# The end of a fused attention and Fourier kernel: when the last output products are made, and on which engine the last sums are

## The chip, the cores and the metric

The kernel runs on one core of one Trainium2 chip. The metric is the device time of one execution in microseconds (us). The kernel before takes 426.28 us (median of 3 runs, 426.26 to 426.36). The page of the profile and all answers of the trace come from one more execution of the same program, taken by the hardware profiler.

## The reference, cut to what matters

One input x of 2048 tokens and 448 features goes through two branches, and a gate mixes them.

```python
# x: (1, 2048, 448), 16 heads of 28 features
g = sigmoid((x * gate_w).sum(-1, keepdims=True))
qkv = (x @ wqkv).reshape(B, S, 3, 16, 28)
p = softmax(q @ k.T * 28 ** -0.5)           # per head, 2048 x 2048
a = (p @ v).reshape(B, S, 448) @ wo
X = rfft2(x.astype(float32))                # over tokens and features
b = irfft2(X * (w_r + 1j * w_i), s=(S, 448)).astype(bfloat16)
return g * a + (1 - g) * b
```

Only the end of the attention branch matters here: the last block of softmax values times v, its scaling by the softmax sum and the gate, its product with wo, and the sum with what is already there of the same output rows (the Fourier branch and the first three groups of heads).

## The kernel before, in words

**Tiling.** The 16 heads are four groups T of four heads. The queries are four blocks of 512. A chunk c is one group with one block of queries: 16 chunks, c = 4 T + block. In every chunk there are 16 blocks of 128 keys. For each of them TensorE makes the scores of four heads (line 829, each head in 32 rows of the array), an engine takes the exponential, and TensorE multiplies the result with v (line 998, each head in 32 columns of the array) into one PSUM bank, `psPV`, which holds four heads of 32 rows (28 features, and in row 28 the softmax sum) times 512 queries. Most exponentials are ScalarE's (line 1077, of two or three PSUM banks at a time, `Pt`); some key blocks are made on VectorE by an integer trick and a polynomial (lines 843 to 895, `Pd`).

**The order of the work.** Every engine runs its own instructions in the order in which the program wrote them. `stream` (line 1330 and on) writes this order: one turn per exponential of ScalarE, with the scores of the turn after next, some value products (`do_pv`), and pieces of all other work where a planner with costs and due times finds room. Ahead of scores it puts a product with zeros (line 1034) into the array rows that the scores leave free.

**The last chunk (c = 15).** Its last four key blocks are handled by parts of the queries: `PARTS` are the queries 0 to 255, 256 to 383 and 384 to 511 (called part 0, 1 and 2). `split` makes a key of each part with two key blocks (part 0, so there are two such keys) or four (parts 1 and 2). Scores and exponentials go part by part. The value product of such a key is lines 989 to 995: 8 matmuls for a key of part 0, 16 for part 1 or 2. In part 2 they are sorted by head; the very last exponential (one bank) holds head 3 of part 2.

When a part's last value product is written, `pv_part` writes its way out: `over` (VectorE: transpose out of PSUM, line 1555; reciprocal of the softmax sum, line 1556; times the gate, line 1557), `scaled` (line 1560, the 32 x 32 blocks times that factor; on GpSimd for part 0, on VectorE for parts 1 and 2) and `back` (line 1565, transposed to `oT`, with head features in the partitions). For part 0 `back` is held until `over` of part 1 is written.

**`tail`.** It writes what the turns left over. Output rows are numbered by tile: tiles 12 to 15 are the last four tiles of 128 rows (e = 0 to 3). Part 0 completes e = 0 and 1, part 1 completes e = 2, part 2 completes e = 3. `last_values` (line 1543) is the product with wo for the last group of heads; `sums` (line 1538) puts the base of a tile (all that was made of these rows before, float32, in `late`) into the bank through a product with the identity, in two passes; `add_base` (line 820) adds the base on VectorE on the way out instead. Ahead of the last key (part 2) `tail` writes `sums` for e = 1 and then `last_values` for e = 0 and 1, and so these products stand on TensorE between the value products of part 1 and of part 2:

```python
                pf = [self.bank(b) for b in (0, 1)]
                self.sums(pf[1], 1)
                for e in (0, 1):
                    self.last_values(pf[e], e, e == 0)
```

After part 2 come `sums` for e = 3, `last_values` for e = 2 and for e = 3. On the way out tile 12 is copied by ScalarE (line 1527) and summed with its base on GpSimd (line 1528), tile 13 is copied by ScalarE (1530), tile 14 is summed on VectorE (820), tile 15 is copied by ScalarE (1533). SyncE's queue stores tiles 12, 13 and 14 in this order, ScalarE's queue tile 15. Then SyncE waits for all stores.

**`do_pv`.** In the turns, line 1431 stops a turn's value products of the last chunk when only one key is left, or when the next one is a key of a part and this turn has already waited for values of VectorE (`waited`).

Of the kernel before, what the change touches and what calls it, by code (L numbers as in the profile page):

```python
# [11 lines left out]
BF16 = mybir.dt.bfloat16  # L12
F16 = mybir.dt.float16
F32 = mybir.dt.float32
U16 = mybir.dt.uint16
ACT = mybir.ActivationFunctionType
ALU = mybir.AluOpType
# [3 lines left out]
P = 128  # L21
S = 2048
D = 448
# [5 lines left out]
F2 = 450  # L29
FCH = 113  # L30
NG = 4
QW = 512
NC = 16
# [36 lines left out]
PARTS = ((0, 256), (256, 128), (384, 128))  # L70
# [92 lines left out]
class Kernel:  # L163
# [817 lines left out]
    def pv(self, c, i, first, last):  # L981
        T = c // 4
        pcs = self.pieces.pop((c, i))
        self.packs -= self.pack_t[(c, i)] is not None
        if not isinstance(i, int):
            q0, w = PARTS[i[1]]
            n = len(i[2:])

            pairs = [(j, h) for j in range(n) for h in range(4)]
            if i[1] == len(PARTS) - 1:  # L990
                pairs.sort(key=lambda jh: jh[1])
            for j, h in pairs:
                self.nc.tensor.matmul(self.psPV[32 * h:32 * h + 32, q0:q0 + w], lhsT=self.vsb[:, i[2 + j], 4 * T + h, :],
                                      rhs=pcs[h][:, w * j:w * j + w], start=False, stop=True,
                                      tile_position=(0, 32 * h), skip_group_check=True)
            return
        for h in range(4):
            self.nc.tensor.matmul(self.psPV[32 * h:32 * h + 32, :], lhsT=self.vsb[:, i, 4 * T + h, :], rhs=pcs[h],  # L998
                                  start=first, stop=last, tile_position=(0, 32 * h))
# [399 lines left out]
    def do_pv(self, k, left, most, limit=0.0):  # L1399
        done = 0  # L1400
        waited = False
        while done < most and self.pv_c < NC:
            c = self.pv_c
            if (self.tp < self.pv_free and not self.ended) or 2 in self.open:
                break
            cand = None
            for i in sorted(left[c], key=lambda i: (i,) if isinstance(i, int) else i):
                if not self.has([f"W{i // 4}" if c < 4 else f"V{i}" if isinstance(i, int) else "V15"]):
                    continue
                if not isinstance(i, int) and any(isinstance(j, int) for j in left[c]):  # L1410
                    break
                if (c, i) not in self.pack_t:
                    continue
                t = self.pack_t[(c, i)]
                if (c, i) in self.shared and not (self.shared[c, i] or 1e9) <= k - 1:
                    continue
                if t is None:
                    if self.pack_tile[(c, i)] <= k - 1:
                        cand = i
                        break  # L1420
                elif c == NC - 1 and not self.free[c] and self.tp < t < limit - 0.4:

                    self.until(t)
                    cand, waited = i, True
                    break
                elif t <= self.tp + (0.0 if self.ring else 0.9):
                    cand = i
                    break
            if cand is None:
                break  # L1430
            if c == NC - 1 and (len(left[c]) == 1 or not isinstance(cand, int) and waited):
                break
            first = not self.pv_open
            left[c].discard(cand)
            last = not left[c]
            if c == NC - 1 and not isinstance(cand, int):
                self.pv_part(cand)
                self.tp += E_PV2 if done else E_PV
                self.add(self.tp, 512)
                done += 1  # L1440
                continue
            self.pv(c, cand, first, last or not any(isinstance(j, int) for j in left[c]))
            self.pv_open = not last
            self.tp += E_PV2 if done else E_PV
            self.add(self.tp, 512)
            done += 1
            if last:
                self.dve(0.75 if c >= TURN else 0.60, at=self.tp + PV)
                self.close_chunk(c)
                self.pv_free = self.tv + VP  # L1450
                self.pv_c += 1
                if self.pv_c < NC:
                    self.psPV = self.psp.tile([P, QW], F32, name="psPV", tag="pv", bufs=1)
                break
# [30 lines left out]
    def tail(self):  # L1485
        nc = self.nc
        left = self.left
        while self.events:
            self.tp = self.tv = max(self.tp, self.tv, self.events[0][0])
            self.run_events()  # L1490
        self.fill_v(1e9)
        assert self.pv_c == NC - 1 and self.epk is None, self.pv_c
        c = NC - 1
        for i in sorted(left[c], key=lambda i: (i,) if isinstance(i, int) else i):
            if len(left[c]) == 1:

                while self.mand or self.open:
                    t = self.ready()
                    assert t < 1e8, self.mand[0][1].name
                    self.tp = max(self.tp, t)  # L1500
                    u = self.pick()
                    if u:
                        if len(u[0].phases) == 1:
                            self.copy = nc.scalar.copy
                        self.step(*u, 1e9)
                    else:
                        self.tp += 0.2
                    self.run_events()
                pf = [self.bank(b) for b in (0, 1)]
                self.sums(pf[1], 1)  # L1510
                for e in (0, 1):
                    self.last_values(pf[e], e, e == 0)
                self.tp = max(self.tp, self.ta + 0.15)
            left[c].discard(i)
            if isinstance(i, int):
                self.pv(c, i, not self.pv_open, not any(isinstance(j, int) for j in left[c]))
                self.pv_open = True
            else:
                self.pv_part(i)
        for n in (3, 2) if self.N % 2 == 0 else (2, 3):  # L1520
            pf.append(self.psp.tile([P, n, QW], F32, name=f"ps{n}", tag=f"ps{n}", bufs=1)[:, 0])
        self.sums(pf[2], 3)
        self.last_values(pf[3], 2, True)
        self.last_values(pf[2], 3)
        fin = [self.rot3.tile([P, F2], BF16, name="X1") for _ in range(3)]
        half = self.rot2.tile([P, QW], F32, name="o32")
        nc.scalar.copy(out=half[:, 0:D], in_=pf[0][:, 0:D])
        nc.gpsimd.tensor_tensor(out=fin[0][:, 0:D], in0=half[:, 0:D], in1=self.base[12], op=ALU.add)
        nc.sync.dma_start(out=self.outv[:, 12, :], in_=fin[0][:, 0:D])
        nc.scalar.copy(out=fin[1][:, 0:D], in_=pf[1][:, 0:D])  # L1530
        nc.sync.dma_start(out=self.outv[:, 13, :], in_=fin[1][:, 0:D])
        self.add_base(pf[3], 14, nc.sync)
        nc.scalar.copy(out=fin[2][:, 0:D], in_=pf[2][:, 0:D])
        nc.scalar.dma_start(out=self.outv[:, 15, :], in_=fin[2][:, 0:D])

    def sums(self, ps, e, a=0):

# [84 lines left out]
```

## Time and profile before

| | |
|---|---|
| median of 3 runs | 426.28 us (426.26 to 426.36) |
| the profiled execution, its own time | 427.39 us |
| its span, first to last instruction | 425.6 us |
| TensorE matmul busy | 406.7 us (96%) |
| ScalarE busy | 411.9 us (97%) |
| VectorE busy | 394.7 us (93%) |
| GpSimd busy | 50.8 us (12%) |
| granted TensorE clock in the 40 slices | 9 tenths or more in all |

How to read it: a busy share is an average over the span. Three engines are busy nearly all the time, and the last 10 us look different from the rest, so they are read by themselves, from the timeline and the chain of waits in a window of the trace. A timeline row has the start in us from the span's start, the time from the first start to the last end of the merged instructions, the engine, the line, and what is written from what; in brackets stands the idle time of the engine before it and who ended it. PEld is the weight load, SPq and ACTq are DMA issues of SyncE and ScalarE. Starts of consecutive instructions of one engine can lie a little before the end of the one ahead, by up to about 0.1 us.

### The profile page before, as it was taken

To read this page: it belongs to the slowest core of one execution; us is meant where nothing else is said; L and a number is where in the kernel's file an instruction comes from. 1 tells how busy PE (TensorE), PEld (TensorE's weight loads), DVE (VectorE), ACT (ScalarE), POOL (GpSimd) and SP (SyncE) were. 2 spreads that over 40 slices of the span, in tenths; PEclk is the share of its full clock that TensorE was granted. 3 is DMA by queue.
4 is the path that set the end of the run, shared out by engine and by line. 5 is a ranking of instruction groups with operands and counts; after the bars stand their busy time and mean duration, and the time that the engine had idled before them with its cause. 6 is when DMAs were issued, how large, how long until landed. Compare 5 with 4: busy or idle time off the path is not lost.

```text
span 425.6 us, 8292 instructions
## 1 busy us (share of the span) xinstructions
PE 406.7 (96%) x3178; PEld 146.1 (34%) x3197; DVE 394.7 (93%) x650; ACT 411.9 (97%) x370; POOL 50.8 (12%) x57
## 2 busy tenths in 40 slices
PE   8999999999999999999999999999999999999995
PEld 5444233333333333333333333333343333333332
DVE  6569989999989999999999999999999999999994
ACT  4899999999999999999999999999999999999994
POOL 6000002020110111011220100202001011110101
PEclk9999999999999999999999999999999999999999
DMA  8900310422302153375664446536453305222132
GB/s 231 183 6 2 8 27 7 113 51 52 77 13 42 31 96 62 74 166 99 144 158 99 108 103 124 103 70 109 109 148 78 76 2 101 56 70 65 32 62 67
DMA packets 32404, 34.30 MB, mean 81 GB/s; under 512 B 14988, under 2 KB 25228, under 8 KB 32332
## 3 DMA queue, kind: packets, MB, share of 16 engines
q1 hardware_dynamic: 28012, 20.21, 20.7%
q0 software_dynamic: 3600, 13.11, 16.9%
q8 instruction: 25, 0.41, 0.4%
q10 hardware_dynamic: 752, 0.44, 0.4%
q14 instruction: 15, 0.12, 0.1%
HBM read 14.85 MB, written 1.95 MB: 39 GB/s over the span
## 4 chain that ended last, share of the span: by engine, by line
PE 35%; ACT 34%; DVE 19%; issue 9%; DMA 2%; SPq 0%; ACTq 0%; DVEq 0%
ACT Pt L1077 29%; PE psPV L998 7%; PE ps L829 6%; DVE Pd L843 4%; PE bg L829 3%; PE psPV L1296 3%; PE bg L288 3%; ACT early L1077 2%; PE bg L1034 2%; DMA xtok<-in_A_x_dram 2%; DVE pa L887 2%; DVE Pd L864 1%; DVE n L861 1%; DVE pa L873 1%; PE bg L673 1%
## 5 line engine op out<-in xcount | busy, mean ns | idle before, releaser
L1077 ACT ACTIVATE Pt<-ps 128x1024 bf16<-128x1024 f32 (+1 forms) x339 | 385.3, 1300 | 0.9 <-PE ps L829 0.4
L829 PE MATMUL ps<-qT,kT 32*128 32x512 bf16 (+2 forms) x926 | 143.7, 375 | 3.7 <-ACT Pt L1077 2.0
L843 DVE TENSOR_SCALAR Pd<-bg 128x512 uint16<-128x512 f32 x130 | 88.6, 682 | 4.8 <-PE ps L829 3.4
L998 PE MATMUL psPV<-Pt,vsb 128*32 128x512 bf16 x818 | 79.9, 388 | 0.0
L829 PEld LDWEIGHTS <-kT 32*128 32x128 bf16 x1056 | 45.7, 91 | 93.9 <-issue 88.9
L829 PE MATMUL bg<-qT,kT 32*128 32x512 bf16 x130 | 49.8, 383 | 0.8 <-DVE Pd L843 0.3
L890 POOL DMA_DIRECT2D Pd<-pa x25 | 24.0, 962 | 218.4 <-PE ps L829 110.6
L887 DVE TENSOR_TENSOR pa<-pa,n 128x2048 uint16<-128x2048 f16 (+2 forms) x33 | 40.4, 1225 | 0.6
L873 DVE TENSOR_TENSOR pa<-pa,n 128x2048 f16<-128x2048 f16 (+1 forms) x33 | 40.3, 1222 | 0.3
L998 PEld LDWEIGHTS <-vsb 128*32 128x32 bf16 x1008 | 23.1, 93 | 50.9 <-issue 50.2
L1296 PE MATMUL psPV<-warm 128*128 128x512 bf16 x124 | 40.1, 385 | 0.0
L1034 PE MATMUL bg<-warm 32*128 32x512 bf16 x92 | 35.3, 383 | 1.8 <-DVE Pd L843 1.4
L975 POOL TENSOR_TENSOR oT<-o,rep 128x512 bf16<-128x512 f32 x13 | 16.4, 1264 | 134.8 <-DVE oT L974 67.0
L288 PE MATMUL bg<-xT,Wg 128*128 128x512 bf16 (+1 forms) x93 | 28.1, 381 | 1.1
L864 DVE TENSOR_SCALAR Pd<-Pd 128x2048 uint16<-128x2048 uint16 (+1 forms) x33 | 24.0, 726 | 0.4
L861 DVE TENSOR_SCALAR n<-Pd 128x2048 uint16<-128x2048 uint16 (+1 forms) x33 | 22.6, 684 | 0.4
L876 DVE TENSOR_SCALAR pa<-pa 128x2048 f16<-128x2048 f16 (+1 forms) x33 | 22.8, 691 | 0.1
L869 DVE TENSOR_SCALAR pa<-n 128x2048 f16<-128x2048 uint16 (+1 forms) x33 | 22.2, 674 | 0.0
L684 DVE CAST U<-bg 128x450 bf16<-128x450 f32 x32 | 19.9, 621 | 2.0 <-PE bg L696 1.2
L1034 PEld LDWEIGHTS <-warm 32*128 32x128 bf16 x92 | 8.3, 91 | 29.0 <-issue 28.2
L1077 ACT ACTIVATE early<-ps 128x1024 bf16<-128x1024 f32 (+1 forms) x13 | 15.2, 1227 | 2.3 <-PE ps L829 2.3
L782 PE MATMUL bg<-Binv,VT 128*128 128x448 bf16 x64 | 16.5, 355 | 0.4 <-DVE fin L792 0.3
(190 smaller groups left out, 431.9 us busy)
## 6 DMA issues: line engine op xcount, KB each, us to landing
Pd<-pa POOLq DMA_DIRECT2D x25, 512.0 KB, 5.0
rep<-rD SPq DMA_DIRECT2D x52, 64.0 KB
CR<-cRB SPq DMA_DIRECT2D x8, 256.0 KB
UT<-U SPq DMA_DIRECT2D x16, 112.5 KB
VT<-U SPq DMA_DIRECT2D x16, 112.5 KB
CR<-cCS SPq DMA_DIRECT2D x8, 192.0 KB
xtok<-in_A_x_dram SPq DMA_DIRECT2D x3, 448.0 KB
out_dram<-fin SPq DMA_DIRECT2D x12, 112.0 KB
```

The lines of the kernel that those rows point to most:

```text
L288: self.nc.tensor.matmul(ps[:], lhsT=self.Wg[T, q][0:k, c, :], rhs=self.xT[0:k, c, 512 * b:512 * b + 512], start=(c == 0), stop=(c == 3))
L829: self.nc.tensor.matmul(out[:, w * j:w * j + w], lhsT=self.kT[T][32 * h:32 * h + 32, 128 * i:128 * i + 128], rhs=self.qT[T][32 * h:32 * h ...
L843: nc.vector.tensor_scalar(out=pk["t"][:, h, :], in0=ps[:], scalar1=SCALE * LOG2E * 512.0, scalar2=127.0 * 512.0, op0=ALU.mult, op1=ALU.add)
L861: v.tensor_scalar(out=st["n"], in0=t, scalar1=511, scalar2=None, op0=ALU.bitwise_and)
L864: v.tensor_scalar(out=t, in0=t, scalar1=127 << 9, scalar2=2, op0=ALU.bitwise_and, op1=ALU.logical_shift_right)
L873: v.tensor_tensor(out=st["a"], in0=st["a"], in1=st["n"], op=ALU.mult)
L887: v.tensor_tensor(out=q, in0=st["a"], in1=st["n"], op=ALU.mult)
L890: nc.gpsimd.dma_start(out=t, in_=q, accum_op=ALU.add)
L998: self.nc.tensor.matmul(self.psPV[32 * h:32 * h + 32, :], lhsT=self.vsb[:, i, 4 * T + h, :], rhs=pcs[h], start=first, stop=last, tile_posi ...
L1034: self.nc.tensor.matmul(ps[:], lhsT=self.warm[sl], rhs=with_free(self.warm[sl], [[0, 4], [1, P]]), start=True, stop=True, tile_position=(3 ...
L1077: self.nc.scalar.activation(out=Pt[:, 0:n, :], in_=ps[:, 0:n, :], func=ACT.Exp, scale=SCALE)
L1296: self.nc.tensor.matmul(self.psPV[:], lhsT=self.warm[:], rhs=with_free(self.warm[:], [[0, 4], [1, P]]), start=False, stop=False, skip_grou ...
```

## The change

Five things change, all at the end of the last chunk.

1. `do_pv`: after a wait for VectorE's values a key of a part is still taken while the planner's TensorE time is not past `limit`. In the written order this moves one key of part 0 (8 matmuls with their weight loads) from behind the last 12-matmul scores (with the product with zeros ahead of them) to in front of both.
2. `tail`: `last_values` for e = 0 and 1 goes from ahead of the last key (part 2) to behind it. `sums` for e = 1 stays ahead of it.
3. `pv`: the last part's 16 value products are written as heads 0 to 2 (key block by key block) and then head 3, instead of head by head.
4. Tile 12: ScalarE's copy and GpSimd's sum are gone; VectorE adds the base directly from PSUM (`add_base`), as its last instruction.
5. The stores: SyncE's queue has tiles 13, 14, 12 in this order; ScalarE's queue tile 15 as before.

All instructions ahead of these, on every engine, stand in the same order in both.

```diff
@@ pv
-            pairs = [(j, h) for j in range(n) for h in range(4)]
-            if i[1] == len(PARTS) - 1:
-                pairs.sort(key=lambda jh: jh[1])
-            for j, h in pairs:
-                self.nc.tensor.matmul(self.psPV[32 * h:32 * h + 32, q0:q0 + w], lhsT=self.vsb[:, i[2 + j], 4 * T + h, :],
-                                      rhs=pcs[h][:, w * j:w * j + w], start=False, stop=True,
-                                      tile_position=(0, 32 * h), skip_group_check=True)
+            def heads(hs):
+                for j, b in enumerate(i[2:]):
+                    for h in hs:
+                        self.nc.tensor.matmul(self.psPV[32 * h:32 * h + 32, q0:q0 + w], lhsT=self.vsb[:, b, 4 * T + h, :],
+                                              rhs=pcs[h][:, w * j:w * j + w], start=False, stop=True,
+                                              tile_position=(0, 32 * h), skip_group_check=True)
+            if i[1] < len(PARTS) - 1:
+                heads(range(4))
+            else:
+                heads(range(3))
+                heads((3,))
@@ do_pv
-            if c == NC - 1 and (len(left[c]) == 1 or not isinstance(cand, int) and waited):
+            if c == NC - 1 and (len(left[c]) == 1 or not isinstance(cand, int) and waited and self.tp > limit):
                 break
@@ tail
                 pf = [self.bank(b) for b in (0, 1)]
                 self.sums(pf[1], 1)
-                for e in (0, 1):
-                    self.last_values(pf[e], e, e == 0)
                 self.tp = max(self.tp, self.ta + 0.15)
...
+        for e in (0, 1):
+            self.last_values(pf[e], e, e == 0)
         for n in (3, 2) if self.N % 2 == 0 else (2, 3):
             pf.append(self.psp.tile([P, n, QW], F32, name=f"ps{n}", tag=f"ps{n}", bufs=1)[:, 0])
         self.sums(pf[2], 3)
         self.last_values(pf[3], 2, True)
         self.last_values(pf[2], 3)
-        fin = [self.rot3.tile([P, F2], BF16, name="X1") for _ in range(3)]
-        half = self.rot2.tile([P, QW], F32, name="o32")
-        nc.scalar.copy(out=half[:, 0:D], in_=pf[0][:, 0:D])
-        nc.gpsimd.tensor_tensor(out=fin[0][:, 0:D], in0=half[:, 0:D], in1=self.base[12], op=ALU.add)
-        nc.sync.dma_start(out=self.outv[:, 12, :], in_=fin[0][:, 0:D])
-        nc.scalar.copy(out=fin[1][:, 0:D], in_=pf[1][:, 0:D])
-        nc.sync.dma_start(out=self.outv[:, 13, :], in_=fin[1][:, 0:D])
+        fin = [self.rot3.tile([P, F2], BF16, name="X1") for _ in range(2)]
+        nc.scalar.copy(out=fin[0][:, 0:D], in_=pf[1][:, 0:D])
+        nc.sync.dma_start(out=self.outv[:, 13, :], in_=fin[0][:, 0:D])
         self.add_base(pf[3], 14, nc.sync)
-        nc.scalar.copy(out=fin[2][:, 0:D], in_=pf[2][:, 0:D])
-        nc.scalar.dma_start(out=self.outv[:, 15, :], in_=fin[2][:, 0:D])
+        nc.scalar.copy(out=fin[1][:, 0:D], in_=pf[2][:, 0:D])
+        nc.scalar.dma_start(out=self.outv[:, 15, :], in_=fin[1][:, 0:D])
+        self.add_base(pf[0], 12, nc.sync)
```

More of the change, by code (lines that the diff above doesn't have):

```diff
@@ L986, in pv @@
             q0, w = PARTS[i[1]]
-            n = len(i[2:])
-            pairs = [(j, h) for j in range(n) for h in range(4)]
-            if i[1] == len(PARTS) - 1:
-                pairs.sort(key=lambda jh: jh[1])
-            for j, h in pairs:
-                self.nc.tensor.matmul(self.psPV[32 * h:32 * h + 32, q0:q0 + w], lhsT=self.vsb[:, i[2 + j], 4 * T + h, :],
-                                      rhs=pcs[h][:, w * j:w * j + w], start=False, stop=True,
-                                      tile_position=(0, 32 * h), skip_group_check=True)
+            def heads(hs):
[7 more added lines that the diff above has]
+            else:
+                assert len(self.tiles[self.N - 1]) == 1
+                heads(range(3))
+                heads((3,))
             return
```

## The prediction

> **What bounds the kernel now.** I read the slices first (no stage stands out until the last two slices), then the chain of waits over the last 30 us, then the timeline of the last 12 us, where all edits lie. The page:
>
> ```profile
> PE 406.7 (96%) x3178; PEld 146.1 (34%) x3197; DVE 394.7 (93%) x650; ACT 411.9 (97%) x370; POOL 50.8 (12%) x57
> ```
>
> From 393 to 414 us the chain runs along ScalarE's exponentials (ACT Pt L1077), with no step between them of over 0.7 us. Then it leaves them:
>
> ```profile
> 413.19 1.03 ACT Pt L1077
> ...
> 415.64 0.39 PE ps L829 x12
> 416.02 0.58 PE psPV L993 x16
> ...
> 417.13 0.43 PE psPV L993 x16
> ...
> 418.75 0.55 PE bg L1543 x2
> 419.30 0.44 PE psPV L993 x16
> ...
> 420.33 0.63 DVE i L1557
> ...
> 422.08 0.53 ACT X L1533
> ```
>
> So from 416 us on the end is a relay of TensorE and VectorE; the exponentials are no longer on it. The timeline has who stands in whose way:
>
> ```profile
> 416.63 0.45 DVE L1555 STREAM_TRANSPOSE ot<-psPV 128x256 f32<-128x256 f32 x1 [0.95 <-PE psPV L993]
> 417.60 0.61 POOL L1560 TENSOR_TENSOR oz<-ot,i 128x256 bf16<-128x256 f32 x1 [13.52 <-DVE i L1557]
> 418.24 0.45 DVE L1565 STREAM_TRANSPOSE oT<-oz 128x256 bf16<-128x256 bf16 x1
> 418.75 0.55 PE L1543 MATMUL bg<-Wo,oT 128*128 128x448 bf16 x2 [0.26 <-DVE oT L1565]
> 418.90 0.31 DVE L1565 STREAM_TRANSPOSE oT<-oz 128x128 bf16<-128x128 bf16 x1
> 419.76 0.32 DVE L1555 STREAM_TRANSPOSE ot<-psPV 128x128 f32<-128x128 f32 x1 [0.55 <-PE psPV L993]
> 419.80 1.13 POOL L1528 TENSOR_TENSOR X<-o,late 128x448 bf16<-128x448 f32 x1 [1.59 <-ACT o L1527]
> 420.33 0.62 DVE L1557 TENSOR_TENSOR i<-i,g 128x4 f32<-128x4 f32 x1
> 422.16 0.33 SPq L821 DMA_DIRECT2D out_dram<-U  x1
> 422.64 0.35 ACTq L1534 DMA_DIRECT2D out_dram<-X  x1
> ```
>
> Three losses are to be seen. (a) The last values (L993 at 419.23) stand behind the two products L1543, which wait until 418.69 for VectorE's transpose of part 0. The last exponential (started 417.66, 0.64 long) was done at 418.30. (b) VectorE waits 0.55 us for these values. (c) VectorE's tiny multiply L1557, 0.17 us in parts 0 and 1, takes 0.62 us and ends at 420.95, just when GpSimd's sum ends (419.80 + 1.13 = 420.93).
>
> That (c) is GpSimd's doing is borne out elsewhere: L639, median 0.23 us, took 0.74 us beside another GpSimd sum, and ended 0.03 us behind it:
>
> ```profile
> 139.50 1.27 POOL L975 TENSOR_TENSOR oT<-o,rep 128x512 bf16<-128x512 f32 x1 [20.75 <-DVE oT L974]
> 140.06 0.74 DVE L639 TENSOR_SCALAR Dm<-Fc,m 128x4 f32<-128x4 f32 x1
> ```
>
> **The change part by part.** I call T the end of VectorE's last transpose (L1565, 421.31 + 0.31 = 421.62). Behind T come the product of tile 15, its copy, and its store (issue 422.64 = T + 1.02; its packets run 423.49 to 424.00, T + 2.38; the span ends 1.6 us later).
>
> *Eight value products ahead of the scores.* The same 8 matmuls are taken from behind the scores. Line 993's sixteen 256-column matmuls start in four rounds, 0.11 us apart ((0.62 - 0.28) / 3), so 8 are 0.23 us. In front: the value products ahead start at 414.92, 0.39 long; eight more push the product with zeros (415.25) to about 415.47. It uses array rows that the scores don't, and at 416.51 the two forms run side by side (L1034 416.51, L829 416.52). The scores start at 415.60 because the exponential that frees their bank (414.10 + 1.46) ends at 415.55; they are covered up to there. Their values are from exponentials that ended by 413.3, so the moved block waits for nothing. If that cover failed altogether, the scores would come 0.2 us later, against 0.3 us between their end (416.02) and the exponential that reads them (416.33): nothing lost. Behind: part 0's transpose L1555 starts 0.22 us earlier (416.41; VectorE idles 0.95 us before it), and with it part 1's products (released by that transpose at 417.08), GpSimd's scaling and both L1565: the second ends at 418.99 instead of 419.21. Taken: -0.22 us for part 1; bounds 0 and -0.23.
>
> *The two products behind the last values.* TensorE then has, after part 1 (issued to 417.25): the sum L1538 (two passes; the next matmul starts 0.38 us after the second's start, as at 420.45), done near 418.1 to 418.2, then the last values. Heads 0 to 2 have their data (exponential ended 417.81), head 3's four matmuls wait for 418.30 + 0.05. They share 32 columns, so I let them run one behind another at 0.05 us each: last start 418.53, end 418.75, VectorE free to read at 418.80 to 418.85. This new wait holds back, on TensorE, the two products, the sum for tile 15 and the products of tiles 14 and 15; see the third rival. VectorE itself is busy until 418.99 with part 1's transpose, and its next instruction can overlap that by 0.07 us (as 421.55 does 421.62). So L1555 of part 2 starts at about 418.95 instead of 419.76: -0.81 us. Bounds: -0.84, and -0.55 if the first edit gives nothing (VectorE then busy until 419.21).
>
> *No sum on GpSimd.* L1557 goes from 0.62 to 0.17 us, and L1560 behind it from 0.29 to 0.25 as in part 1: -0.45 to -0.49; taken -0.48 (the chain from L1555 to L1565 was 1.86 us, part 1's instructions with the same gaps make 1.38). The lower bound without L1560 and a little start effect is -0.44. ScalarE's copy of tile 12 goes too: it lay in an idle stretch, nothing.
>
> So T moves by -0.81 - 0.48 = -1.29 us, to 420.33; bounds -0.99 and -1.34.
>
> *Heads 0 to 2, then 3.* Head by head already had head 3 last; the 16 took 0.44 us in part 2 and 0.41 in part 1's order. Nothing; at most 0.05 us either way, under VectorE's 0.1 us.
>
> *Tile 12 on VectorE, last, and the new order of stores.* Tile 14's sum starts when its product is there (next paragraph: about 420.3) at 420.35, 0.58 long; the next PSUM read can start 0.08 us before that ends (two casts at 414.53 took 1.15 together), so tile 12's sum ends at 421.43 and SyncE issues its store at 421.46; tile 14's store was issued 0.5 us before and does not hold it up (an issue is 0.33). Tile 15's store is issued at 420.33 + 1.02 = 421.35. So two stores start within 0.11 us, where the four of before start 0.43 us or more apart. Each store's packets in these windows:
>
> ```profile
> 421.78:422.24 0.46, 0.26 (x1) 0.00 (x0) 0.35 (x1) 0.16 (x1) 0.00 (x0) 1.00 0.81 247
> 422.99:423.46 0.47, 0.00 (x0) 0.00 (x0) 0.00 (x0) 0.00 (x0) 0.00 (x0) 1.00 0.71 244
> ```
>
> (the last two columns are the DMA engines' busy share and GB/s). A store takes 0.46 to 0.51 us alone at 70 to 80% of all 16 engines, so two together need between 0.51 (they overlap freely) and 0.97 us (one after the other); by busy share 2 x 0.47 x 0.70 = 0.66, and some 0.1 for uneven engines: 0.77. Tile 15's packets start at 422.20 (issue + 0.85), so the last ends at 422.97 instead of 424.00; bounds 422.76 (tile 12's alone: issue + 1.30, as tile 14's before) and 423.17. The Trainium skill speaks against hoping for free overlap here (DMA: Bandwidth & Descriptors, Issuing engines are not separate DMA queues): stores of different queues run on the same 16 DMA engines and interleave. By the figure of about 358 GB/s to HBM in its Specifications a second 112 KB would add 0.32 us to tile 15's end at 422.71, as an estimate, and the sum would end at 423.03. No two stores coincide in this trace.
>
> **Sum.** 424.00 - 422.97 = 1.03 us off the span: 425.6 to 424.6. The profiled execution took 427.39 us with that span, the median run 426.28, 1.11 less; a saving at the end carries over unchanged, so 426.28 - 1.03 = 425.25. Bounds: -0.99 on T with the worst pairing of the stores (0.46 later against T than before) saves 0.53, giving 425.75; -1.34 with free overlap (0.05 later) saves 1.29, giving 425.0.
>
> **The rivals.**
>
> *The last stores take it back.* Tile 12 was stored first, 1.7 us before the end; now its sum and its store come last. For it: the stores' busy shares; against it: no row with two at once. With full serialization and no gain by the moved block: 425.75; with only one of the two 425.45 to 425.5. The middle, some 425.6, is within 0.2% of before (0.85 us).
>
> *TensorE's backlog becomes the bound.* Behind head 3 stand two products (0.2 us each, 0.15 behind its last start, as the sum at 419.60 behind the values), the sum (0.48 and 0.38) and tile 14's product (0.19): from 418.53 to about 420.15, when tile 15's product can start. It needs oT at 420.33, so 0.2 us are left. If head 3 runs 0.4 us later than I put it, the end moves by 0.2, and tile 14's sum (already bound by TensorE, 420.3) with tile 12's store by the whole 0.4: 425.65. For it: the products did run in TensorE's idle time before; against it: the slack.
>
> *Slower: a longer end without an earlier start.* If L1557's delay is not GpSimd's, or VectorE's start is bound elsewhere, so that T stays at 421.62, then tile 12's sum ends at T + 1.01 and its store meets tile 15's: T + 1.87 + 0.77 to 0.97 instead of T + 2.38, which is 0.26 to 0.46 us later: 426.55 to 426.75. It decides as soon as T gains under 0.26 us. Against it: the last values have been ready to run since 418.35, and L639. A loss over 0.2% needs the exponentials late besides.
>
> *No effect of the moved block alone* is inside the bounds above.
>
> **Chances.** The forecast, 425.0 to 425.4: 0.60, all faster by over 0.2%. The stores take it back: 0.20, mostly within 0.2%. TensorE's backlog: 0.12, within for three quarters. The slower end: 0.08, over half of it beyond 0.2%. So faster by over 0.2% 0.63, within 0.2% 0.32, slower by over 0.2% 0.05; 0.2% is about what a measurement of this kernel can tell from no change. The range for 8 in 10 takes in the bounds and the first two rivals, with 0.1 us for what the rows round away: 424.9 to 425.85.
>
> **What would show it.** Right: part 0's L1555 near 416.4; the last values starting before 418.3 with a pause before head 3; the last multiply by the gate at 0.17 us; the last transpose ending near 420.3; two overlapping bursts of packets ending near 423.0. Wrong: an exponential with a gap before it after 415 us; VectorE still idle before its last read of PSUM; tile 15's product waiting for TensorE instead of VectorE; the last packets later than 423.2.

## The result, and the profile after

The changed kernel takes 425.32 us (median of 8 runs, 425.24 to 426.86), the kernel before 426.63 us beside it (8 runs, 426.19 to 428.09). The ratio is 0.9969, with a 95% interval of 0.9955 to 0.9984: faster by 0.31%. The whole interval lies below 1, but its near end, 0.16%, falls short of the 0.2% that the forecast named. A second set of runs of the same two gave 0.9974 (0.9964 to 0.9984), with medians of 425.95 and 426.82 us. The forecast was 425.25 us.

These runs of one kernel differ by up to 2 us, and in the profiled executions this arises ahead of the change. In that of before TensorE waited 0.83 us for a piece of the input at 10.6 us; in that of the changed kernel it did not. The two rows, before and after:

```profile
10.63 0.65 PE L296 MATMUL bg<-ident,xtok 128*112 128x128 bf16 x8 [0.83 <-DMA xtok<-in_A_x_dram]
9.48 0.61 PE L296 MATMUL bg<-ident,xtok 128*112 128x128 bf16 x8
```

From 12 us on the exponentials of the two executions stand 1.18 to 1.19 us apart, up to the last one. So the spans of these two executions (425.6 and 423.5 us) must not be subtracted. What can be compared is the stretch behind a common point. I take the start of the last exponential (one bank, 0.64 us long): 417.66 us before, 416.48 us after. In all executions shown here the last six exponentials start at the same distances from it, within 0.01 us. From that point the span ends 7.95 us later before, and 6.98 us later after: 0.97 us saved. The lowest times of the runs, 426.19 and 425.24, differ by 0.95 us.

Page of the changed kernel (span and busy shares):

```profile
span 423.5 us, 8289 instructions
PE 406.2 (96%) x3178; PEld 146.1 (35%) x3197; DVE 394.6 (93%) x651; ACT 411.4 (97%) x369; POOL 49.6 (12%) x56
```

The busy times hardly move; a share of the span could not have shown this change. Its chain of waits, from the place where it leaves the exponentials:

```profile
413.08 0.41 PE ps L829 x8
413.49 0.32 PE psPV L1300
413.81 0.33 PE psPV L1002 x4
414.14 0.22 PE psPV L990 x8
414.36 0.28 PE bg L1038
...
415.73 0.43 PE psPV L990 x16
416.16 0.02 issue
416.19 0.33 DVE ot L1556
...
417.29 0.18 DVE oz L1561
417.48 0.02 issue
417.50 0.31 DVE oT L1566
417.81 0.21 DVE ot L1556
...
418.26 0.17 DVE i L1558
...
419.09 0.56 DVE U L820
```

From 416.19 us on it is VectorE alone, one instruction behind another: the products L1543 and the late value products that stood in the chain before are gone, and it ends in VectorE's sums instead of ScalarE's copy. The timeline of the same stretch (line numbers are up by one from the tail on, and L993 is now L990):

```profile
415.23 0.45 DVE L1556 STREAM_TRANSPOSE ot<-psPV 128x256 f32<-128x256 f32 x1 [0.73 <-PE psPV L990]
417.02 0.54 PE L990 MATMUL psPV<-Pt,vsb 128*32 128x128 bf16 x16
417.49 0.55 PE L1544 MATMUL bg<-Wo,oT 128*128 128x448 bf16 x2
417.50 0.31 DVE L1566 STREAM_TRANSPOSE oT<-oz 128x128 bf16<-128x128 bf16 x1
417.74 0.27 DVE L1556 STREAM_TRANSPOSE ot<-psPV 128x128 f32<-128x128 f32 x1
418.26 0.16 DVE L1558 TENSOR_TENSOR i<-i,g 128x4 f32<-128x4 f32 x1
418.78 0.31 DVE L1566 STREAM_TRANSPOSE oT<-oz 128x128 bf16<-128x128 bf16 x1
419.02 0.62 DVE L820 TENSOR_TENSOR U<-ps,late 128x448 bf16<-128x448 f32 x1
419.56 0.61 DVE L820 TENSOR_TENSOR U<-bg,late 128x448 bf16<-128x448 f32 x1
419.67 0.86 SPq L821 DMA_DIRECT2D out_dram<-U  x2
420.11 0.37 ACTq L1534 DMA_DIRECT2D out_dram<-X  x1
```

VectorE reads part 2 (417.74) while its last transpose of part 1 is still ending (417.50 + 0.31); the idle 0.55 us ahead of this read are gone. The multiply L1558 is 0.16 us long. The two issues of SyncE end at 420.53, so the last store (tile 12) is issued at 420.20, 0.09 us behind tile 15's. The DMA engines in the stretch of the pair and in that of tile 14's store alone (busy share and GB/s last):

```profile
421.00:421.78 0.78, 0.00 (x0) 0.00 (x0) 0.00 (x0) 0.00 (x0) 0.00 (x0) 0.87 0.86 294
420.50:420.97 0.47, 0.00 (x0) 0.00 (x0) 0.00 (x0) 0.00 (x0) 0.00 (x0) 1.00 0.72 244
```

The pair needs 0.77 us, more than one store and less than two.

### The profile page after: what moved, and what is told of

The parts are those of the page before. It is cut to its first block, busy times and chain, and to the rows that moved or that the text cites. A ratio compares the mean times of both kernels' runs of the same rounds, so it can differ in the third digit from the quotient of the medians.

```text
span 423.5 us, 8289 instructions
## 1 busy us (share of the span) xinstructions
PE 406.2 (96%) x3178; PEld 146.1 (35%) x3197; DVE 394.6 (93%) x651; ACT 411.4 (97%) x369; POOL 49.6 (12%) x56
## 4 chain that ended last, share of the span: by engine, by line
PE 37%; ACT 34%; DVE 19%; issue 9%; DVEq 0%; ACTq 0%
ACT Pt L1081 30%; PE psPV L1002 7%; PE ps L829 6%; DVE Pd L843 4%; PE bg L829 4%; PE psPV L1300 3%; PE bg L288 3%; ACT early L1081 2%; PE bg L1038 2%; DVE pa L887 2%; DVE Pd L864 1%; DVE n L861 1%; DVE pa L873 1%; PE bg L673 1%; DVE U L684 1%
```

## The experiments

The first three columns of the table are us from the start of the last exponential, in one profiled execution each. "Part 2 read" is the start of the last transpose out of PSUM (L1555 in the kernel before), "T" the end of VectorE's last transpose. The ratio is to the kernel before, beside which the runs were made.

| kernel | part 2 read | T | span end | ratio (95% interval) |
|---|---|---|---|---|
| before | 2.10 | 3.96 | 7.95 | |
| before, only tile 12 on VectorE | 2.10 | 3.50 | 7.96 | 0.9998 (0.9989 to 1.0008) |
| before, only the products behind the last values | 1.47 | 3.80 | 7.79 | 0.9997 (0.9988 to 1.0006) |
| before, only the block ahead of the scores | 1.88 | 3.74 | 7.74 | 1.0007 (0.9990 to 1.0024) |
| changed kernel | 1.25 | 2.61 | 6.98 | 0.9969 (0.9955 to 0.9984) |
| changed, the block behind the scores | 1.48 | 2.83 | 7.28 | 0.9986 (0.9977 to 0.9996) |
| changed, head by head | 1.26 | 2.61 | 7.01 | 0.9975 (0.9964 to 0.9986) |
| changed, tile 12 left out (its rows stay unwritten) | 1.26 | 2.61 | 6.66 | 0.9969 (0.9957 to 0.9981) |
| changed, tile 12 on GpSimd again | 1.25 | 2.61 | 7.36 | 0.9982 (0.9970 to 0.9994) |
| the same, stores in order 13, 14, 12 | 1.25 | 2.60 | 7.15 | 0.9980 (0.9971 to 0.9990) |
| the same, tile 15 out in halves | 1.25 | 2.61 | 7.02 | 0.9979 (0.9967 to 0.9990) |
| changed, once more | 1.25 | 2.61 | 7.03 | 0.9974 (0.9964 to 0.9984) |
| changed, bases of 12, 13 and 15 in bfloat16 through TensorE | 1.25 | 2.61 | 6.61 | 0.9970 (0.9959 to 0.9981) |
| the same, 14 too, 15 in two banks | 1.25 | 2.61 | 6.44 | 0.9965 (0.9950 to 0.9981) |

The intervals are as wide as the single effects, since the time ahead of the last exponential differs by up to 2.5 us between executions (it starts at 416.48 us in the changed kernel's, at 418.94 in that with the block alone). So the small differences below are read from the table's columns, and the changed kernel's own two executions (6.98 and 7.03) say that these repeat within 0.05 us.

**One edit at a time.** Tile 12 on VectorE alone:

```diff
-        nc.gpsimd.tensor_tensor(out=fin[0][:, 0:D], in0=half[:, 0:D], in1=self.base[12], op=ALU.add)
...
+        self.add_base(pf[0], 12, nc.sync)
```

> The kernel before with only one edit: tile 12 is summed on VectorE, last, and stored last by SyncE's queue; no sum on GpSimd. All times from the start of the last exponential (one bank) in the profiled execution; before: the last transpose of VectorE ends at 3.96, the span at 7.95. Theory (GpSimd's sum blocks VectorE's multiply): the multiply by the gate of part 2 takes 0.17 us instead of 0.62, the last transpose ends at 3.48, and the paired stores of tiles 12 and 15 give 0.38 of it back, as in the changed kernel: span end 7.85, some 426.2 us. Rival (the multiply is long for another reason): last transpose at 3.96 and span end at 8.33, some 426.65 us.

The last multiply, and the end, in the timeline of this kernel:

```profile
419.88 0.16 DVE L1554 TENSOR_TENSOR i<-i,g 128x4 f32<-128x4 f32 x1
420.40 0.31 DVE L1562 STREAM_TRANSPOSE oT<-oz 128x128 bf16<-128x128 bf16 x1
421.14 0.61 DVE L820 TENSOR_TENSOR U<-bg,late 128x448 bf16<-128x448 f32 x1
421.73 0.38 ACTq L1530 DMA_DIRECT2D out_dram<-X  x1
```

The multiply goes from 0.62 to 0.16 us and T from 3.96 to 3.50, as the theory has it; the rival falls. But the span ends at 7.96: the stretch from T to the end grows from 3.99 to 4.46 us, 0.1 more than I expected, and takes back all of it. Alone this edit brings the end nothing.

The products behind the last values alone:

```diff
                 self.sums(pf[1], 1)
-                for e in (0, 1):
-                    self.last_values(pf[e], e, e == 0)
...
+        for e in (0, 1):
+            self.last_values(pf[e], e, e == 0)
```

> The kernel before with only one edit: the products of tiles 12 and 13 behind the last values. Theory: VectorE reads part 2 at 1.5 instead of 2.1 (all from the start of the last exponential), but the tile 12 product, ScalarE's copy and GpSimd's sum follow at about 1.0, 1.3 and 1.9, so GpSimd's sum (1.13 us) starts just ahead of the multiply by the gate (2.04), which then lasts until about 3.05: the last transpose ends near 3.69 instead of 3.96, span end 7.68. So most of the earlier start is lost to GpSimd. Rival (no blocking): last transpose at 2.9, span end 6.9.

Timeline of this kernel:

```profile
418.60 0.27 DVE L1555 STREAM_TRANSPOSE ot<-psPV 128x128 f32<-128x128 f32 x1
419.12 0.16 DVE L1557 TENSOR_TENSOR i<-i,g 128x4 f32<-128x4 f32 x1
419.31 1.13 POOL L1528 TENSOR_TENSOR X<-o,late 128x448 bf16<-128x448 f32 x1 [1.63 <-ACT o L1527]
419.32 1.27 DVE L1560 TENSOR_TENSOR oz<-ot,i 128x128 bf16<-128x128 f32 x1
```

Part 2 is read 0.63 us earlier, and 0.16 us of that are left at T. GpSimd's sum moves along with the products that feed it. Here the multiply L1557 just gets through, and the scaling L1560 (0.29 us otherwise) starts 0.01 us behind GpSimd's sum, takes 1.27 us and ends 0.15 us after it. I had expected the multiply to be the victim; that it is the scaling hangs on 0.02 us, by which the multiply ends ahead of GpSimd's sum. T and the end are 0.11 us later than expected.

The block ahead of the scores alone:

```diff
-            if c == NC - 1 and (len(left[c]) == 1 or not isinstance(cand, int) and waited):
+            if c == NC - 1 and (len(left[c]) == 1 or not isinstance(cand, int) and waited and self.tp > limit):
```

> The kernel before with only one edit: eight value products of part 0 ahead of the last 12-matmul scores. Theory: no exponential comes later (gaps between them as before, overlaps of 0.1 to 0.15 us), part 0's transpose and all behind it come 0.22 us earlier, GpSimd's sum as well, so the blocked multiply keeps its length: last transpose 3.74 instead of 3.96, span end 7.73 instead of 7.95 from the start of the last exponential. Rival (the block delays the scores): a gap of up to 0.2 us ahead of the exponential of the last 12-matmul scores, and an end that is not earlier.

T and the end are 0.22 us earlier, to 0.01 us as expected, and none of the last six exponentials moved. The blocked multiply keeps its 0.62 us. The ratio of this kernel (1.0007) does not show the gain: its runs reach 429.04 us, and its profiled execution lost about 1.4 us near 303 us, where the granted clock of TensorE was 0.51 from 303 to 306 us (1.00 in the changed kernel's).

The three alone save 0.00, 0.16 and 0.22 us, under 0.4 in all. Together they save 0.97. So most of the gain belongs to no edit alone. It belongs to two of them together: the next kernel has those two without the block.

**One edit taken back.** The block behind the scores again:

```diff
-            if c == NC - 1 and (len(left[c]) == 1 or not isinstance(cand, int) and waited and self.tp > limit):
+            if c == NC - 1 and (len(left[c]) == 1 or not isinstance(cand, int) and waited):
```

> The changed kernel with the eight value products of part 0 behind the last 12-matmul scores again. Theory: VectorE is busy with part 1 for 0.22 us longer, and so its read of part 2 and all behind it come 0.2 to 0.25 us later: span end 7.2 from the start of the last exponential (6.98 with the block in front). Rival (part 2's read is bound by the last exponential, so the block brings nothing): 6.98.

T is 0.22 us later and the end 0.30. So the block is worth 0.22 us at T in both places where it was tested. The pair of the other two, alone, saves 7.95 - 7.28 = 0.67 us, where each alone saved 0.00 and 0.16: one starts part 2 earlier, the other keeps GpSimd from holding it up there.

The value products head by head again:

```diff
-                heads(range(3))
-                heads((3,))
+                for h in range(4):
+                    heads((h,))
```

> The changed kernel with the last part's 16 value products head by head again (head 3 is last in both). Theory: VectorE's transpose of part 1 bounds the read of part 2, so nothing: span end within 0.05 us of 6.98 from the start of the last exponential. Rival (head by head is slow on TensorE, 0.05 us per matmul one behind another): the values of heads 0 to 2 take 0.6 us instead of 0.2, head 3 starts 0.2 to 0.3 us later, and the end comes 0.1 to 0.2 us later.

The read of part 2 and T are the same within 0.01 us, the end within 0.03. The edit does nothing that can be measured here.

Tile 12 left out:

```diff
-        self.add_base(pf[0], 12, nc.sync)
```

> The changed kernel without the sum and the store of tile 12, whose 128 output rows stay unwritten: what the last sum and the paired store cost. Theory (two stores together need more than one): tile 15's packets, 0.65 us in the changed kernel, take 0.46 to 0.5, and the span ends at 6.7 to 6.8 from the start of the last exponential instead of 6.98. Rival (stores overlap freely): 6.95 to 6.98.

The span ends at 6.66, 0.32 us before the changed kernel's, a little more than expected. Tile 15's store, issued at the same 3.63, ran its packets in 0.45 us instead of 0.65. This is what the last sum and the meeting of the stores cost.

**Tile 12 on GpSimd again,** all else as in the changed kernel:

```diff
+        nc.scalar.copy(out=half[:, 0:D], in_=pf[0][:, 0:D])
+        nc.gpsimd.tensor_tensor(out=fin[0][:, 0:D], in0=half[:, 0:D], in1=self.base[12], op=ALU.add)
+        nc.sync.dma_start(out=self.outv[:, 12, :], in_=fin[0][:, 0:D])
...
-        self.add_base(pf[0], 12, nc.sync)
```

> The changed kernel with tile 12 on ScalarE's copy, GpSimd's sum and SyncE's first store again, as before the change; all other edits stay. From the start of the last exponential, in the changed kernel: tile 12's product ends at 1.37, part 2's scaling runs from 1.97 to 2.26, last transpose ends at 2.61, span end 6.98. Theory: ScalarE copies until 1.95, GpSimd could start at 2.03, 0.06 behind VectorE's scaling, which has its two inputs first: GpSimd then runs beside or behind it, the last transpose stays near 2.6, tile 12 is stored before tile 15, no stores coincide, and the span ends at 6.7 to 6.85, earlier than the changed kernel. Rival (whoever starts, VectorE waits for GpSimd's sum): scaling until 3.1 to 3.2, last transpose 3.5, span end near 7.5.

```profile
419.11 0.29 DVE L1564 TENSOR_TENSOR oz<-ot,i 128x128 bf16<-128x128 f32 x1
419.20 1.19 POOL L1532 TENSOR_TENSOR X<-o,late 128x448 bf16<-128x448 f32 x1 [1.73 <-ACT o L1531]
419.68 0.62 DVE L820 TENSOR_TENSOR U<-ps,late 128x448 bf16<-128x448 f32 x1
420.42 0.33 SPq L1533 DMA_DIRECT2D out_dram<-X  x1
420.77 0.37 ACTq L1538 DMA_DIRECT2D out_dram<-X  x1
420.84 0.38 SPq L1535 DMA_DIRECT2D out_dram<-X  x1
421.32 0.40 SPq L821 DMA_DIRECT2D out_dram<-U  x1
```

Half right. VectorE's scaling starts 0.09 us ahead of GpSimd's sum and keeps its 0.29 us; T is 2.61, as without GpSimd. The end is not earlier but 0.38 us later. SyncE's queue had tile 12's store first: it waited until 420.42 for GpSimd, and tile 14's, whose sum was done at 420.30, was issued third, at 421.32. I had left out that queue's order. With the order 13, 14, 12:

```diff
-        nc.sync.dma_start(out=self.outv[:, 12, :], in_=fin[0][:, 0:D])
...
         self.add_base(pf[3], 14, nc.sync)
+        nc.sync.dma_start(out=self.outv[:, 12, :], in_=fin[0][:, 0:D])
```

> The changed kernel with tile 12 by ScalarE's copy and GpSimd's sum, but with SyncE's stores in the order 13, 14, 12, so that tile 14's store does not wait behind tile 12's. From the start of the last exponential: last transpose 2.61; stores issued: 13 at 2.45, 14 at 3.2, 12 at 3.57, 15 (ScalarE) at 3.63. Theory (the end of the run with GpSimd's sum back was SyncE's queue, whose last store was issued at 4.18): the last packets end near 5.2, span end 6.8 to 6.9, 0.1 to 0.2 us before the changed kernel (6.98) and 0.5 before the run with the stores in the old order (7.36). Rival (GpSimd's sum costs something else at the end): 7.2 or more.

The end comes 0.21 us earlier than with the old order, but at 7.15, not at 6.8 to 6.9. Tile 12's and tile 15's stores are now issued 0.005 us apart, and the last packets end at 5.40, later than in the changed kernel (5.29), though the last issue is 0.1 us earlier. From these to the span's end it takes 1.76 us instead of 1.69. So in neither of the two orders is GpSimd's sum a better place for tile 12 than VectorE's.

Tile 15 copied out in halves by two engines:

```diff
-        nc.scalar.copy(out=fin[2][:, 0:D], in_=pf[2][:, 0:D])
+        nc.scalar.copy(out=fin[2][:, 0:D // 2], in_=pf[2][:, 0:D // 2])
+        nc.vector.tensor_copy(out=fin[2][:, D // 2:D], in_=pf[2][:, D // 2:D])
```

> The same, and tile 15 is taken out of PSUM in halves of 224 columns, by ScalarE and by VectorE, which is free after tile 14. Theory: the two halves are done near 3.45 instead of 3.60, tile 15's store is issued at 3.48, and the stores of tiles 12 and 15 end near 5.1: span end 6.7 to 6.8. Rival (the stores' packets bound the end): no gain against the run with the stores in the order 13, 14, 12.

```profile
421.18 0.35 ACT L1537 CAST X<-ps 128x224 bf16<-128x224 f32 x1 [0.65 <-PE ps L1548]
421.56 0.39 DVE L1538 CAST X<-ps 128x224 bf16<-128x224 f32 x1 [0.28 <-ACT X L1537]
```

VectorE's half did not run beside ScalarE's: its row names ScalarE's copy as what it waited for. The two read the same PSUM bank and write the same tile; which of these makes it wait is not shown. So the question of the expectation was not put, and tile 15's store was issued later (3.87). Still the end, 7.02, is 0.13 us ahead of the run that this one builds on. The last packets end at 5.40 in both; from there to the span's end it takes 1.62 us here and 1.76 there.

The changed kernel once more, beside these:

> The changed kernel once more, beside the two others on the same chip: span end 6.98 from the start of the last exponential, 425.3 us.

**A version that beats both.** What is left in the changed kernel is VectorE's second sum and the meeting of two stores. Both go if tile 12 is finished early. Its base can go through TensorE like tile 13's, but not in the two float32 passes (about 0.86 us) that TensorE has no room for. So the bases of tiles 12, 13 and 15 are kept in bfloat16, which rounds them; this version does not compute quite the same:

```diff
+        ... 12 + i: self.late[i] if i == 2 else self.late[i].bitcast(BF16)[:, 0:D] ...
...
-        ... lhsT=self.Fc[:, P + 8:P + 8 + P], rhs=self.base[12 + e][:, a:D] ...
+        ... lhsT=self.ident[:], rhs=self.base[12 + e][:, a:D] ...
...
+                self.sums(pf[0], 0)
                 self.sums(pf[1], 1)
...
+        nc.scalar.copy(out=fin[0][:, 0:D], in_=pf[0][:, 0:D])
+        nc.sync.dma_start(out=self.outv[:, 12, :], in_=fin[0][:, 0:D])
...
-        self.add_base(pf[0], 12, nc.sync)
```

> The changed kernel with the bases of tiles 12, 13 and 15 kept in bfloat16 and put into their PSUM banks by one-pass products with the identity; tile 12 gets such a sum too (ahead of the last values), is copied out by ScalarE ahead of tile 13, and stored first. VectorE sums only tile 14. Theory: a one-pass sum costs TensorE about 0.2 us instead of 0.86, the last transpose stays at 2.61 from the start of the last exponential, tile 15's store (issued at 3.63) meets no other, as in the run without tile 12: span end 6.65 to 6.7, 425.0 us, 0.3 us before the changed kernel. Rival (the end is bound by something else in the full kernel, TensorE's backlog or SyncE's queue): 6.9 or more.

The end is at 6.61, 0.04 us before what was expected; the run without tile 12 had 6.66. Then tile 14 the same way, and tile 15 as two products of 224 columns in two banks and copied to two tiles, so that the copies need not wait for each other:

```diff
+        for ps, a in ((pf[2], 0), (pf[4], h)):
+            self.nc.tensor.matmul(ps[:, 0:h], lhsT=self.oT[3][:, 128 * 15:128 * 15 + 128], rhs=self.Wo[:, 3, a:a + h], start=False, stop=True)
...
+        nc.scalar.copy(out=two[0][:, 0:h], in_=pf[2][:, 0:h])
+        nc.scalar.dma_start(out=self.outv[:, 15, 0:h], in_=two[0][:, 0:h])
+        nc.vector.tensor_copy(out=two[1][:, 0:h], in_=pf[4][:, 0:h])
+        nc.sync.dma_start(out=self.outv[:, 15, h:D], in_=two[1][:, 0:h])
```

> The same, with tile 14 by such a sum and ScalarE's copy as well, and tile 15 as two products of 224 columns in two banks, taken out by ScalarE and by VectorE at once and stored as two stores of 56 KB from both queues. Theory: the halves are copied by 3.3 and 3.5 from the start of the last exponential, the stores are issued at 3.35 and 3.5, span end 6.45 to 6.6. Rival (two stores of 448-byte rows need as long as one of 896-byte rows, 0.5 us, and collide): 6.65 or more.

```profile
419.63 0.40 SPq L1541 DMA_DIRECT2D out_dram<-X  x1
419.74 0.35 ACT L1543 CAST U<-ps 128x224 bf16<-128x224 f32 x1 [0.16 <-PE ps L1534]
419.84 0.39 DVE L1545 CAST U<-pv 128x224 bf16<-128x224 f32 x1 [0.46 <-PE pv L1534]
420.12 0.40 ACTq L1544 DMA_DIRECT2D out_dram<-U  x1
420.26 0.33 SPq L1546 DMA_DIRECT2D out_dram<-U  x1
```

Now the copies do run side by side, and the end is at 6.44: 1.51 us before the kernel before, 0.54 before the changed kernel. Its runs have a median of 424.88 us and a lowest time of 424.66 (changed kernel: 425.24). The ratios of the two to before do not part them (their intervals overlap); the column of span ends does.

## Why the prediction was right, point by point

Times of the changed kernel are shifted here by 1.18 us, the distance of the two last exponentials, so that they can be set beside the forecast's.

- *The block ahead of the scores*: -0.22 us; part 0's transpose started at 415.23 + 1.18 = 416.41 as forecast, at no cost to the exponentials. Shown by the runs with it alone and without it.
- *The products behind the last values*: the read of part 2 was put at 418.95, bound by VectorE's transpose of part 1; it started at 417.74 + 1.18 = 418.92. Of the sixteen matmuls four, taken here to be head 3's, start 0.055 us apart, the first 0.05 us behind the last exponential's end and the last at 418.52 (forecast 418.53). VectorE was still busy with part 1, so these did not bound the read.
- *No sum on GpSimd*: the multiply went to 0.16 us. L1561 stayed at 0.29 instead of 0.25, and the transpose before it gained 0.04; the chain took 1.35 us for 1.38. T came to 420.27 for 420.33.
- *Heads 0 to 2, then 3*: nothing, shown.
- *Tile 12 last, and the stores*: two stores issued 0.09 us apart (forecast 0.11), 0.77 us for their packets (forecast 0.77), last packet at 422.95 (422.97). Of the forecast 0.77 only 0.66 came from the busy shares; the 0.1 for uneven engines was a guess that no row gave, and that it fits to 0.01 us is luck. By the figure of the Trainium skill (DMA: Bandwidth & Descriptors, Specifications) the sum gave 423.03; the trace is 0.08 us under that. Small misses cancel: T came 0.06 us earlier than forecast, and tile 15's first packet 0.90 us after its issue instead of 0.85. What is left is the stretch from the last packet to the span's end, which took 1.69 us instead of 1.62. So 0.97 us were saved where the sum said 1.03.
- *The rivals.* The stores took back 0.38 us of what T gained (1.35 to 0.97), where the sum had 0.26 (1.29 to 1.03), and not all of it. TensorE's backlog did not become the bound: tile 15's product waited 0.16 us for VectorE's transpose (forecast 0.2 us of slack). The slower end did not come, but its mechanism is real: in the run with tile 12's sum moved alone T gained 0.46 us and the end nothing. The forecast put the price of the longer end at 0.26 to 0.46 us and its turning point at the lower of the two; measured it is 0.47, of which 0.29 lie up to the last packet and 0.18 behind it.

That the median, 425.32 us, fell 0.07 us from the forecast is partly luck. The kernel before had 426.63 us beside it and not the 426.28 from which the forecast counted, and in the second set the changed kernel's median, 425.95, lay outside the stated range. What the prediction had right is the saving: 1.03 forecast, 0.97 from the traces, 1.31 and 0.87 between the medians of the two sets.

What the prediction did not see is that the edits are not a sum. It worked them out in the order of the text, each on top of the ones before, and that came out right. Taken alone, the products behind the last values bring 0.16 us and not the 0.6 by which part 2 starts earlier, because GpSimd's sum follows them.

## What to carry to other kernels

At the end of a kernel follow one thread of instructions to the last store, and count from a common event near the end when two executions are compared; what the input's arrival added at the start (1.19 us between the two executions here) is larger than the change. An edit that takes a wait away should be tested together with whatever is late next: here two edits worth 0.00 and 0.16 us alone were worth 0.67 together. And the last stores should be counted as work of their own: tiles finished at the same time meet on the DMA engines, and a store that waits in a queue holds up the ones behind it.

## What the runs showed of the hardware that was not expected

- In these runs an instruction of VectorE with two SBUF inputs was blocked by GpSimd's sum when it started behind it, and not when it started ahead. The scaling, 0.01 us behind, ended 0.15 us after GpSimd's sum (1.27 us instead of 0.29). The reciprocal, with one such input, kept its 0.18 us beside the same sum in the kernel before. When the scaling started 0.09 us ahead it was not slowed, and GpSimd's sum ended 0.99 us after it, 1.19 instead of 1.13 us long: GpSimd lost only 0.06 us, so it was not held up for the whole of VectorE's instruction. The Trainium skill (SBUF — State Buffer, SBUF: two separate sides) calls the port pair that these two engines share an exclusive lock held for the whole instruction. The first of these cases agrees; in the second GpSimd's row starts before it needs the port, or the lock is not that strict, and these runs don't tell which.
- Two stores of 112 KB from two queues, issued 0.09 us apart, need 0.77 us for their packets, one alone 0.45 to 0.51. Tile 15's packets begin 0.86 to 0.90 us after its issue when it is alone or 0.09 us apart, 0.99 at 0.05 us (tile 12 moved alone, and the changed kernel without the block), 1.02 at 0.005 us. But in the run with tile 15 in halves they also begin 0.99 us after it, with the other issue 0.26 us ahead, so the distance of the issues alone does not decide it.
- From the last packet to the span's end it took 1.61 to 1.80 us. With tile 12 moved alone and with the block behind the scores, the last packet ends 2.67 us behind T, as in the changed kernel (2.68), and this last stretch is 1.80 and 1.78 us instead of 1.69. That is the 0.1 us by which those two ends were later than expected; what decides it is not shown.
- Two stores of 56 KB with rows of 448 bytes needed 0.32 to 0.33 us each, and the last packet of the run ended 0.23 us before that of the run with one store of 112 KB. The copies ahead of them were split as well.
